# Another written-out order for a kernel of attention and a two-layer product on one core

## The chip, the cores and the metric

The kernel runs on one core of a Trainium2 chip. The metric is device time in microseconds (us) of one execution; a run gives one such time, and a kernel is compared by the median of its runs. The engines of the core are named as in the profile: PE (TensorE matmul, PEld its weight loads), DVE (VectorE), ACT (ScalarE), POOL (GpSimd) and SP (SyncE, which here only issues DMAs).

## The reference

Four batches of eight heads, 768 positions, 64 values a head. Heads 0, 2 and 6 attend causally to everything before them; the other five keep only the first four keys and a window of 64. The attention's output, with the heads side by side, is 3072 rows of 512, and goes through a two-layer product with a slope for negative values:

```
scores = scale * np.matmul(q, k.transpose(0, 1, 3, 2))
...
a = np.exp(scores)
a = a / (np.sum(a, axis=-1, keepdims=True) + 1e-09)
return np.matmul(a, v).astype(np.float32)
...
h = x @ w_in                                      # 512 -> 2048
g = np.maximum(h, 0.0) + alpha * np.minimum(h, 0.0)
return (g @ w_out).astype(np.float32)             # 2048 -> 512
```

## The kernel before

**Units of work.** The heads go two at a time: pair n = 0 to 15 is a batch (n // 4) and two heads of it. The third pair of a batch (n % 4 = 2) has one causal and one windowed head, the last (n % 4 = 3) two windowed ones. Each step of a pair is an item with a name, and the program is one long list of these names, `ORDER` (line 14). The kernel defines all items and then calls them in the order of the list; nothing else schedules. Each engine, and each engine's DMA queue, works its own items off strictly in that order, and waits (on semaphores) where an input or a buffer is not ready. A suffix /V, /A or /P puts an item on DVE, ACT or POOL in place of its default engine.

**The names.** For pair n, with head hh where there are two parts:

- `Lq`, `Lk`, `Lv` load q, k and v to SBUF (lines 189 to 205). All are issued by SP but for one k load, which ACT issues. A q or k load of batch 0 is one head, 128 x 384 float32 (192 KB), in packets of 1.5 KB; a v load is two to five DMAs in packets of 256 bytes, since a row of v is 64 floats.
- `C` casts q and k to bf16 (L323), `Cv` casts v (L328). In batch 0, `T` transposes on PE and `tq`, `tk` copy the result from PSUM. In later batches `tq` and `tk` are transposes of 32 x 32 blocks on DVE, `Dm` parks the result in device memory (L338, four DMAs), and `Dq`, `Dk` fetch it back in the layout that the scores need (L342 to L352); `dk` copies the four first keys.
- `S` are the score matmuls (L442), `s` the exponentials on ACT (L486, L527, L530), `m` the masks by multiplication, `A` the products with v (L556), `a` the division (L565, L566), `X` and `x` the transpose and copy to `xT` (L581).

For block t of the rows (two blocks a batch, 512 and 256 rows): `P` is the first product (L603), `p` and `g` its activation on ACT and DVE (L608, L615), `O` the second product (L623), `o` the copy and the store. `P` of block 0 needs `x` of all four pairs of batch 0, and is cut in parts for its first columns: `P0.4.0` and `P0.5.0` need `x0` and `x1` alone.

`wi0` to `wi7` load w_in as eight DMAs of 64 partitions and 512 columns, `wo0` to `wo3` load w_out as four. These cast from float32 on the way, and POOL issues them on a queue of its own, which the profile names software_dynamic (q0); SP's is q1, hardware_dynamic:

```
def load_w_in(n):
    hh, lo = n % 2, n // 2 * 512
    nc.gpsimd.dma_start(w_in_b[D * hh:D * hh + D, :, lo:lo + 512],
                        dram(moe_w_in, 4 * D * hh * d_ff + lo, [[d_ff, D], [D * d_ff, 4], [1, 512]]))
```

The first columns of `P0` read `wi2` and `wi3`, the next ones `wi4` and `wi5`. Each of POOL's DMAs signals on one of eight semaphores in turn, so the first w_out load can be issued when the first w_in load has landed, the second after the second, and so on. SP's DMAs likewise: each is issued once the one eight before it has landed.

**Warm-up.** `warm` items are matmuls on zeros that only keep PE busy. `Al` turns the slopes on PE.

**Staging.** While PE works on `P` and `O` of batch b, the other engines and PE between these prepare and run the attention of batch b + 1. Only the attention of batch 0 has nothing beside it: until its four `x` are there PE has no `P` to do.

Of the kernel before, what the change touches and what calls it, by code (L numbers as in the profile page):

```python
# [11 lines left out]


ORDER = """
busz busy Lk0.1 kz1 kx1 Lq1.0 warm13 warm10 kx3 warm9 warm4 warm11 Lk0.0 warm1 vo id La Al C0.0.1/P Lk1.0 ey ky1
warm16 Lq0.0 or os1 C0.0.0 Lq0.1 T0.0 C0.1.1/A C0.1.0/A T0.1 m12.1.2 C1.0.0 warm0 tq0.0/V tk0.0/A Lq3.0 warm14 zero st
tq0.1 tk0.1 warm17 Lk2.1 S0.1.2 Lq2.0 warm6 s0.1.2 one Lk2.0 S0.0.2 S0.0.0 s0.0.2 al C2.0.0 S0.1.0 sz1 os2 S0.1.1
Lq3.1 S0.0.1 s0.0.0 s0.0.1 Lq1.1 Lk1.1 s0.1.0 C1.1.0/V T1 tq1/V tk1 Lv3 Lq2.1 S1.0.0 Cv3.1/V s1.0.0 C2.1.0/V T2 Lv0
Cv3.0/V m8.0.2 S1.0.1 s0.1.1 S1.1.0 Cv0/A kx2 s1.0.1 S1.1.1 Lk3.0 tk2.0 tq2 S2.0.0 C3.0.0/A tk2.1 Lq5 nmr s1.1.1
s1.1.0 Lv2 A0.0 Cv2.0 wi3 ky2 kz2 sz2 warm2 ky3 a0.0 S2.0.2 S2.1.0 Lk3.1 C3.1.0 Cv2.1 s2.0.0 T3 wi4 Lv1 Cv1/A tq3 A0.1  # L20
wi2 s2.1.0 S2.0.1 sz0 tk3 wi5 s2.0.2 kz3 S3.1.0 a0.1 s2.0.1 S2.1.1 s2.1.1 A1.1 A2.0 a1.1 A1.0 a1.0 S3.1.1 S3.0.0
s3.1.0 S3.0.1 s3.1.1 s3.0.0 a2.0 A3.1 A2.1 s3.0.1 X1 x1/A Lk5 A3.0 C5.0.0 a3.1 a2.1 X0 warm5 x0 a3.0 warm15 X2 P0.5.0
wi7 X3 x3 x2/A P0.7 P0.9 p0.7 g0.7 p0.9 P0.8 P0.6 g0.9 P1.6 p1.6 g1.6 p0.6 g0.6 P0.10 C5.1.0 tk5 p0.10 P0.11 Lq4 wi1
wi6 p0.11 P0.14 g0.10 tq5 p0.14 g0.14 g0.11 Lk4 P0.13 P0.4.0 P0.5.1 P0.5.2 p0.5 g0.5 Lk7 P1.8 wi0 P0.4.1 P0.4.2 p1.8
P0.12 P0.0.0 P0.0.1 p0.8 g0.8 wo0 g1.8 Lq7 p0.12 g0.12 P0.3.0 P0.0.2 p0.4 P0.3.1 P0.3.2 p0.3 warm8 P0.2.0 C4.0.0
P0.2.1 P1.12 wo1 P0.1.0 Dm5 g0.4 Dq5 P0.1.1 P0.1.2 Dk5 C4.1.0/V nms warm7 p0.13 g0.13 P1.4 g0.3 tq4 tk4 Dm4 P1.10 p0.1
g0.1 C7.1.0/A P1.2 wo2 p0.0 P0.2.2 C7.0.0/V p1.2 g0.0 Dk4 P0.15 Lk6 g1.2 p0.2 g0.2 tk7 P1.14 wo3 P1.0 p1.0 p1.14
O0.3.0 O0.1.0 O0.1.1 Dq4 g1.0 m14.0.2 Lq6 g1.14 p1.10 O0.3.1 tq7 Dm7 p1.12 p1.4 dk5/A S5.0.1 S5.1.2 g1.10 g1.4 O0.3.2
O0.2.0 O0.2.1 O0.2.2 Lv5 s5.1.2 O1.1.0 p0.15 g0.15 S5.1.0 g1.12 S5.0.0 S5.0.2 s5.0.2 O0.2.3 s5.0.0 o0.2/V m5.0.2
s5.1.0 O0.1.2 S4.1.1 S4.1.3 C6.1.0/V S4.0.0 s4.0.0 C6.0.0/V s4.1.1 m4.1.1/P s4.1.3 O0.1.3 m4.0.0/P o0.1 tk6 O0.3.3  # L30
o0.3 tq6 m5.0.0 S4.1.2 S4.0.3 s4.0.3 O0.0.0 S4.1.4 S5.1.1 s4.1.2 m5.1.0 S4.0.1 S4.0.5 Cv5/V s5.0.1 m5.0.1 warm3 m5.1.2
Lv4 s4.0.1 s4.1.4 m4.1.4/P O1.1.1 O1.1.2 s5.1.1 m5.1.1 S4.0.4 S4.1.0 S4.0.2 S4.1.5 s4.1.5 m4.1.5 A5.0 O1.1.3 A5.1 a5.0
m4.0.3 a5.1 Dk7 s4.0.2 O0.0.1 s4.1.0 dk7/P Dq7 S7.1.0 S7.0.2 m4.1.0/P S7.0.1 s4.0.5 S7.0.0 s4.0.4 m4.0.5 o1.1 Dm6
S7.1.2 S7.1.1 Lv7 s7.1.1 s7.1.2 m7.1.2 m7.1.1 Cv4/V m4.0.1/P Dq6 O1.0.0 O1.0.1 s7.1.0 Dk6.0 Dk6.1 dk6/P warm12 s7.0.0
s7.0.1 m4.0.4 O0.0.2 m7.0.0 A4.0 X5 S6.0.1 s7.0.2 S6.0.3 S6.0.4 Cv7 s6.0.1 O1.0.2 a4.0 m6.0.1 x5 S6.1.0 S6.0.2 S6.1.1
m7.1.0 s6.0.4 m6.0.4 s6.0.3 m6.0.3 m4.1.3/P Lq8 S6.1.2 m7.0.1 m7.0.2 S6.0.0 S6.0.5 s6.1.0 s6.1.1 m6.1.0/P Lv6 s6.0.2
A7.1 Cv6.0/P Lk8 a7.1 s6.0.0 m6.0.0/P Lq9 Lq10 A4.1 s6.0.5 a4.1 A7.0 a7.0 O1.0.3 s6.1.2 m6.0.5/P A6.0 X7 Lk9 m6.1.1 X4
m6.1.2 Cv6.1/A A6.1 O0.0.3 x7/A a6.0 a6.1 X6 C8.0.0/V x6 C8.1.0/V tk8 x4/A P2.0 tq8 P2.1 p2.1 P3.2 g2.1 C9.1.0/V P2.15
C9.0.0/V P2.7 p2.15 P3.10 o0.0/V g2.15 o1.0 tq9 P3.12 tk9 P3.6 Dm8 p3.2 p3.12 g3.12 p3.6 g3.6 Lq11 g3.2 P2.3 p2.3 Lk10
g2.3 C10.1.0 C10.0.0/A tk10 P2.9 p2.9 g2.9 p2.0 P3.4 p3.4 P2.4 p2.4 m8.1.2 g2.0 g3.4 p2.7 P2.5 g2.4 P2.13 P3.0 P2.12  # L40
g2.7 p2.13 g2.13 Dm9 tq10 p2.5 Dq8 P2.14 p2.14 g2.14 Lk11 C11.1.0 g2.5 P2.2 Dk8 P2.10 p2.2 g2.2 C11.0.0 tk11 P2.6 Lv9
Lq13 P2.8 O2.2.0 Dk9 p2.6 Dq9 p2.10 p2.8 g2.6 P2.11 p2.11 g2.10 O2.0.0 O2.0.1 g2.8 O2.2.1 tq11 g2.11 O2.0.2 O2.2.2
p3.10 p2.12 Lv10 Lv11 Cv9/P Dm11 p3.0 g3.10 dk9/A S9.1.0 S9.0.2 g3.0 S9.0.0 S9.0.1 S9.1.1 g2.12 Lk13 S9.1.2 s9.1.2
C13.1.0/V m9.1.2/P O2.2.3 s9.0.0 Lq12 s9.1.1 s9.0.2 O2.0.3 s9.1.0 m9.1.0/P o2.0/V s9.0.1 m9.0.1 P3.8 o2.2 S8.0.1
S8.1.5 S8.0.0 S8.0.5 S8.1.3 S8.1.4 p3.8 O2.1.0 s8.1.3 Lk12 O2.1.1 O2.1.2 Lv8 s8.0.5 m8.0.5 g3.8 O2.1.3 Dk11 C13.0.0/A
s8.1.5 m9.0.2/P s8.0.0 S8.0.3 S8.0.4 S8.1.2 m9.0.0 S8.0.2 tq13 S8.1.0 s8.1.4 m8.1.4/P s8.0.1 m8.0.1 S8.1.1 Dq11 dk11/P
O3.1.0 m8.0.0 Cv8/A m9.1.1/P s8.0.4 s8.0.2 o2.1/V A9.0 P3.14 s8.1.2 a9.0 s8.0.3 Dm10 m8.0.4/P Dq10 m8.0.3/P s8.1.1
m4.0.2 s8.1.0 A9.1 S11.0.1 a9.1 S11.1.1 S11.1.0 p3.14 g3.14 S11.0.0 S11.0.2 Cv11/P Dk10.0 tk13 O3.1.1 s11.0.0 s11.0.1
A8.0 C12.0.0/V O3.1.2 Dk10.1 S10.0.3 s11.1.1 dk10 S10.1.0 S10.0.1 Lk15 s11.1.0 s11.0.2 m11.1.0 S11.1.2 C12.1.0/A
S10.0.0 Dm13 S10.1.2 m11.0.1 O3.1.3 s10.0.3 s10.0.1 s10.1.2 a8.0 s11.1.2 s10.1.0 m11.1.1 O3.0.0 m10.0.1 m10.0.3  # L50
S10.1.1 s10.0.0 m10.0.0 m11.1.2 Lq15 S10.0.4 m8.1.1/P S10.0.5 S10.0.2 s10.0.5 m11.0.0/P C15.1.0/A s10.1.1 O3.0.1
s10.0.4 m8.1.0/P m10.1.0 Cv10.0 A11.1 a11.1 s10.0.2 m10.1.1 m8.1.5/P m8.1.3/P A8.1 m11.0.2 O3.0.2 O3.0.3 A11.0 a8.1
Cv10.1/A X9 X8 Lv13 x9/A Cv13/A Lv15 O2.3.0 m10.1.2 A10.1 a11.0 m10.0.4/P m10.0.5/P A10.0 O2.3.1 a10.1 a10.0 O2.3.2 x8
X11 X10 x10/A O2.3.3 x11 tk12 P5.12 tq12 Dm12 o2.3/V C15.0.0/V tk15 P4.8 P4.13 o3.0/V P4.0 Lk14 o3.1 P4.15 p4.15 g4.15
Lq14 P4.10 p4.10 g4.10 p4.8 P4.2 p4.2 tq15 C14.0.0 P4.14 g4.8 p4.0 g4.0 P4.9 C14.1.0 Dk13 P4.1 p4.13 g4.13 p4.1 g4.2
P4.3 p4.3 g4.3 P4.12 g4.1 P4.7 p4.7 g4.7 p4.14 g4.14 P4.5 p5.12 g5.12 p4.5 g4.5 P4.4 p4.4 P5.0 Dq12 g4.4 Dq13 p4.9
g4.9 P4.6 P4.11 p4.12 P5.10 tq14 g4.12 dk13/A Dk12 p4.6 g4.6 p4.11 O4.3.0 g4.11 O4.2.0 O4.2.1 O4.2.2 O4.2.3 p5.0 g5.0
p5.10 S13.0.0 S13.0.1 S13.1.1 S13.0.2 S13.1.2 O4.3.1 O4.3.2 O4.3.3 s13.0.2 s13.1.2 g5.10 s13.0.1 Dm15 Dk15 m10.0.2
dk15/A S12.0.1 S12.1.5 S12.0.0 s13.1.1 tk14 S13.1.0 s13.0.0 s13.1.0 P5.6 m13.1.0/P o4.3/V p5.6 P5.4 p5.4 O4.1.0
s12.0.0 O4.1.1 s12.1.5 O4.1.2 m13.1.2 S12.1.1 m13.0.2 S12.0.2 g5.6 S12.0.3 g5.4 s12.0.1 S12.0.4 S12.1.3 o4.2/V S12.0.5  # L60
m13.0.1 Cv15/P m12.0.0 S12.1.0 s12.0.5 m12.0.5/P s12.0.3 s12.0.2 O4.1.3 m13.0.0 A13.0 O4.0.0 o4.1/V s12.0.4 m13.1.1
s12.1.1 m12.0.4 s12.1.0 a13.0 s12.1.3 Dm14 Dq15 m12.0.3 m12.0.1 m12.1.0 O4.0.1 Dq14 S15.0.0 Lv12 S15.1.1 S15.0.1
S15.0.2 S15.1.2 m4.1.2 Dk14.1 S15.1.0 dk14 Cv12/P A13.1 s15.1.2 s15.0.2 m15.1.2 a13.1 s15.1.0 s15.1.1 m15.1.1 s15.0.1
s15.0.0 O4.0.2 O4.0.3 m12.1.3/P Dk14.0 A12.0 o4.0/V S12.1.4 X13 S12.1.2 S14.0.0 S14.0.3 a12.0 P5.2 P5.14 x13 P5.8
s14.0.3 p5.2 g5.2 s14.0.0 m14.0.0 m15.0.0 s12.1.2 p5.14 g5.14 O5.0.0 O5.0.1 p5.8 g5.8 Lv14 S14.0.4 Cv14.1/P S14.0.1
S14.1.0 m12.1.1 S14.0.5 s12.1.4 Cv14.0/A m15.0.2 m12.1.4/P m12.1.5 S14.1.2 S14.0.2 S14.1.1 s14.1.1 s14.0.2 O5.0.2
s14.0.1 m15.1.0 s14.1.2 m14.0.1 m14.1.1/P A15.1 A12.1 s14.1.0 m14.1.0/P m15.0.1 A15.0 a12.1 m14.0.3/P a15.1 a15.0
s14.0.4 m14.0.4 m14.1.2/P O5.1.0 s14.0.5 O5.1.1 O5.1.2 A14.1 a14.1 m12.0.2 m14.0.5/P A14.0 a14.0 O5.1.3 X15 X12 X14
x12/A x15/A O5.0.3 x14 P6.12 P6.8 p6.12 g6.12 o5.1 p6.8 P7.6 g6.8 P6.11 p6.11 P6.0 P6.1 p6.1 o5.0 g6.1 p7.6 g7.6 P7.4
P6.3 g6.11 P6.14 P7.10 p6.0 g6.0 p7.10 p6.3 P6.6 p6.6 g6.3 g6.6 P6.4 p6.4 p7.4 g7.4 P6.10 p6.14 P6.2 g6.14 p6.2 g6.4  # L70
g6.2 P6.13 P6.9 g7.10 P6.15 p6.9 g6.9 P6.7 p6.15 g6.15 p6.7 g6.7 m6.0.2 P7.14 p6.10 P7.12 P6.5 p6.5 g6.5 O6.3.0 O6.2.0
# [753 lines left out]
```

## Time and profile before

| | us |
|---|---|
| median of 3 runs | 243.77 (242.94 to 243.86) |
| the profiled execution, its own time | 241.82 |
| its span, first to last instruction | 240.1 |
| PE busy in the span | 223.3 (93%) |
| DVE, ACT, POOL busy | 160.6, 137.4, 62.0 |
| PE busy from 0 to 34 us | 26.2 of 34 |
| PE busy from 34 to 127 us | 91.0 of 93 |
| PE busy from 127 to 139 us | 9.7 of 12 |
| PE busy from 139 to 240.1 us | 96.5 of 101.1 |

The table says where a different order can change the time: PE is the engine that is nearly always busy, and what it lacks lies mostly in the first 34 us, with a smaller piece from 127 to 139 us. In the first 34 us it is busy with warm-up too, and partly at a lower clock.

### The profile page before, as it was taken

What the parts mean: (1) busy time and instruction counts of PE and PEld (TensorE: products, weight loads), DVE (VectorE), ACT (ScalarE), POOL (GpSimd) and SP (SyncE); (2) the same over time, 40 slices, a digit from 0 to 9 for tenths busy, and PEclk for the clock granted to TensorE, in tenths of its full rate; (3) what the DMA queues carried; (4) which work ended last, traced back from release to release, by engine and by line L of the source; (5) the groups of instructions that cost most, each with busy time, mean ns of one, the idle gap of its engine ahead of it and who ended that gap; (6) DMA issues with size and microseconds to landing.
All of it is one profiled execution on the core that took longest, in us unless ns stands there. A gap on an engine that the chain in (4) does not pass through costs nothing. (4 is left out here: it accounts for less than half of the span.)

```text
span 240.1 us, 5361 instructions
## 1 busy us (share of the span) xinstructions
PE 223.3 (93%) x1990; PEld 130.3 (54%) x2019; DVE 160.6 (67%) x393; ACT 137.4 (57%) x276; POOL 62.0 (26%) x112
## 2 busy tenths in 40 slices
PE   7778789999999989999998899999999999999993
PEld 2567645575445657544464454454557655456543
DVE  3854555998385898997578576994878654674410
ACT  3476845665386754863998542684587555645101
POOL 2506981000053222140765113120442611000000
PEclk9976999999999999999999999999999999999999
DMA  6999999956998875999977906943761002000222
GB/s 227 289 250 194 289 223 205 207 106 151 273 266 232 204 252 147 308 228 224 296 231 188 209 9 164 310 87 76 199 159 46 0 3 87 1 3 0 98 90 76
DMA packets 65523, 39.67 MB, mean 165 GB/s; under 512 B 48905, under 2 KB 63705, under 8 KB 65497
## 3 DMA queue, kind: packets, MB, share of 16 engines
q1 hardware_dynamic: 59305, 30.01, 49.7%
q0 software_dynamic: 5728, 8.91, 16.2%
q10 hardware_dynamic: 464, 0.40, 0.5%
q8 instruction: 16, 0.26, 0.5%
q14 instruction: 10, 0.08, 0.1%
HBM read 32.50 MB, written 11.01 MB: 181 GB/s over the span
## 5 line engine op out<-in xcount | busy, mean ns | idle before, releaser
L603 PE MATMUL P<-xT,w_in_b 128*128 128x256 bf16 (+1 forms) x503 | 85.3, 325 | 1.5 <-DMA w_in_b<-in_moe_w_in_dram 0.9
L615 DVE SCALAR_TENSOR_TENSOR g<-neg,oma,P 128x256 bf16<-128x256 f32 (+1 forms) x128 | 70.9, 608 | 21.6 <-ACT neg L608 21.3
L623 PE MATMUL P<-w_out_b,g 128*128 128x512 bf16 x350 | 83.7, 379 | 1.3 <-issue 0.5
L608 ACT ACTIVATE neg<-P 128x512 f32<-128x512 f32 x96 | 54.8, 601 | 42.1 <-PE P L603 33.6
L603 PEld LDWEIGHTS <-w_in_b 128*128 128x128 bf16 x512 | 49.6, 98 | 35.8 <-issue 2.5
L623 PEld LDWEIGHTS <-g 128*128 128x128 bf16 x368 | 33.7, 98 | 37.5 <-issue 1.6
L486 ACT ACTIVATE eR<-P 128x448 bf16<-128x448 f32 (+1 forms) x63 | 33.9, 616 | 7.9 <-PE P L442 7.2
L527 ACT ACTIVATE eS<-P 128x368 bf16<-128x368 f32 (+1 forms) x55 | 26.3, 526 | 16.1 <-PE P L442 15.1
L442 PE MATMUL P<-qT,kT 64*128 64x184 bf16 (+7 forms) x272 | 25.2, 256 | 5.3 <-DVE kT L406 1.2
L631 POOL DMA_DIRECT2D out_dram<-ot x18 | 11.5, 639 | 62.9 <-DVE ot L629 46.0
L442 PEld LDWEIGHTS <-kT 64*128 64x128 bf16 x272 | 14.0, 96 | 15.8 <-issue 8.8
L566 DVE TENSOR_TENSOR xn<-P,rcp 128x384 bf16<-128x384 f32 x32 | 17.8, 558 | 1.6 <-PE P L442 0.5
L629 DVE COPY ot<-P 128x512 f32<-128x512 f32 x13 | 8.9, 682 | 14.9 <-PE P L623 14.9
L332 DVE STREAM_TRANSPOSE mid<-nat 128x384 f32<-128x384 f32 x24 | 16.3, 705 | 0.1
L498 POOL TENSOR_TENSOR eR<-eR,mr 128x128 bf16<-128x128 bf16 x27 | 11.7, 447 | 16.2 <-issue 8.2
L538 DVE TENSOR_TENSOR eS<-eS,ms 128x368 bf16<-128x368 bf16 x35 | 11.7, 348 | 5.3 <-ACT eS L527 5.3
L538 POOL TENSOR_TENSOR eS<-eS,ms 128x368 bf16<-128x368 bf16 x10 | 8.9, 889 | 22.6 <-ACT eS L527 22.6
L565 DVE RECIPROCAL rcp<-P 128x6 f32<-128x6 f32 x32 | 6.1, 190 | 9.6 <-PE P L556 9.6
L556 PE MATMUL P<-vb,eS 124*128 124x65 bf16 x240 | 10.6, 193 | 1.3 <-DVE eS L538 1.1
L323 POOL CAST nat<-qkf 128x768 bf16<-128x768 f32 x8 | 7.9, 998 | 15.0 <-DMA qkf<-in_q_dram 7.1
L581 ACT COPY xT<-P 128x768 bf16<-128x768 bf16 x8 | 6.2, 800 | 9.7 <-PE P L442 8.7
L556 PEld LDWEIGHTS <-eS 124*128 124x128 bf16 x240 | 9.2, 97 | 4.0 <-DVE eS L538 1.3
(78 smaller groups left out, 167.4 us busy)
## 6 DMA issues: line engine op xcount, KB each, us to landing
qkf<-in_q_dram SPq DMA_DIRECT2D x12, 384.0 KB
qkf<-in_k_dram SPq DMA_DIRECT2D x12, 384.0 KB
mem<-mid SPq DMA_DIRECT2D x48, 96.0 KB
out_dram<-ot POOLq DMA_DIRECT2D x18, 256.0 KB, 4.0
vf<-in_v_dram SPq DMA_DIRECT2D x19, 210.0 KB
vf<-in_v_dram SPq DMA_DIRECT2D x12, 192.0 KB
qT<-mem SPq DMA_DIRECT2D x12, 192.0 KB
w_in_b<-in_moe_w_in_dram POOLq DMA_DIRECT2D x8, 256.0 KB, 10.5
```

The source lines that it names most:

```text
L332: nc.vector.transpose(words.rearrange("p (w r i) -> p i w r", w=4, i=3), nat[n].bitcast(fp32)[:, S // 2 * x:S // 2 * (x + 1)])
L442: fn(to, x, y, **dict(zip(("start", "stop"), flags)))
L486: nc.scalar.activation(ebuf[n, hh][:, lo:hi].rearrange("p (x c) -> p x c", x=len(parts)), banks(got)[:, 0:len(parts), 0:(hi - lo) // len(p ...
L498: by(n, hh, m).tensor_tensor(ej, ej, mr, op=ALU.mult)
L527: nc.scalar.activation(slots_of(n, hh, m), sc[:, :, 0:2 * WIDE].rearrange("p x (s c) -> p x s c", c=WIDE), AF.Exp, scale=scale)
L538: by(n, hh, m).tensor_tensor(slots, slots, ms[:, first:first + 2 * len(x), :], op=ALU.mult)
L556: nc.tensor.matmul(pav[:, i, :], e[0:rows, o:o + 128], vv[0:rows, j, hh, 0:D + 1], start=(m == 0), stop=(m == len(terms) - 1))
L566: nc.vector.tensor_tensor(in_pairs(xn[n], hh, 3), pav[:, :, 0:D, :], rcp.to_broadcast([128, 3, D, 2]), op=ALU.mult)
L603: nc.tensor.matmul(psg[:, w * i:w * (i + 1)], w_in_b[:, c, 128 * fb:128 * (fb + 1)], xT[:, c, o:o + w], start=(x == 0), stop=(x == 3))
L608: nc.scalar.activation(neg[t, f], bank(held["P", t, f][0]), AF.Relu, scale=-1.0)
L615: nc.vector.scalar_tensor_tensor(g_buf[t % 2][:, fb, 0:w], neg[t, f][:, c], oma[:, fb:fb + 1], bank(got[0])[:, c], op0=ALU.mult, op1=ALU.add)
L623: nc.tensor.matmul(bank(held["O", t, s][0]), g_buf[t % 2][:, f, 128 * s:128 * (s + 1)], w_out_b[:, f, :], start=(f == 0), stop=(f == 15))
```

## The change

Only the list `ORDER` changes, in nearly all its lines; the items, their instructions and their shapes are the same. What it amounts to in each queue up to the start of `P0`:

SP issues, before: Lk0.1 Lq1.0 Lk1.0 Lq0.0 Lq0.1 Lq3.0 Lk2.1 Lq2.0 Lk2.0 Lq3.1 Lq1.1 Lk1.1 **Lv3** Lq2.1 Lv0 Lk3.0 Lq5 **Lv2** Lk3.1 Lv1 Lk5 Lq4 Lk4 Lk7 Lq7.
After: Lk1.1 Lk0.1 Lq0.0 Lq0.1 Lq2.0 Lq1.1 Lq2.1 Lk2.0 Lk1.0 Lq3.0 Lk2.1 Lq1.0 **Lv2** Lk3.1 Lk3.0 Lq3.1 Lv0 Lv1 Lq5 **Lv3** Lk5 Lq4 Lk4, then the first park, Lq7 Lk7.

POOL, before: C0.0.1 C1.0.0 st C2.0.0 nmr Cv2.0 **wi3** C3.1.0 Cv2.1 **wi4 wi2 wi5** C5.0.0 **wi7** C5.1.0 **wi1 wi6 wi0** wo0 C4.0.0 wo1 nms wo2 wo3.
After: st C2.0.0 C1.1.0 C2.1.0 nmr Cv2.0 **wi4 wi3 wi2 wi0 wi1 wi5 wi6 wi7** wo1 wo0 wo2 wo3 C7.1.0 nms.

ACT's casts of v, before: Cv0 after s0.1.1 and Cv1 after s2.0.0. After: none of these two (both on DVE), but tq3 and Cv3.0 between s1.1.0 and s2.0.2.

PE: `Al` comes first, ahead of all warm-up matmuls. Ahead of `X3` stand P0.4.0, P0.5.0 and P0.4.1, before it was P0.5.0 alone.

In later batches `Dm10`, `Dq10` and the q and k loads of batch 3 stand further ahead of their readers, and the cast C15.1.0 goes from ACT to POOL and behind the attention of batch 2. The core of the diff:

```diff
-busz busy Lk0.1 kz1 kx1 Lq1.0 warm13 warm10 kx3 warm9 warm4 warm11 Lk0.0 warm1 vo id La Al C0.0.1/P Lk1.0 ey ky1
...
-Cv3.0/V m8.0.2 S1.0.1 s0.1.1 S1.1.0 Cv0/A kx2 s1.0.1 S1.1.1 Lk3.0 tk2.0 tq2 S2.0.0 C3.0.0/A tk2.1 Lq5 nmr s1.1.1
-s1.1.0 Lv2 A0.0 Cv2.0 wi3 ky2 kz2 sz2 warm2 ky3 a0.0 S2.0.2 S2.1.0 Lk3.1 C3.1.0 Cv2.1 s2.0.0 T3 wi4 Lv1 Cv1/A tq3 A0.1
-wi2 s2.1.0 S2.0.1 sz0 tk3 wi5 s2.0.2 kz3 S3.1.0 a0.1 s2.0.1 S2.1.1 s2.1.1 A1.1 A2.0 a1.1 A1.0 a1.0 S3.1.1 S3.0.0
-s3.1.0 S3.0.1 s3.1.1 s3.0.0 a2.0 A3.1 A2.1 s3.0.1 X1 x1/A Lk5 A3.0 C5.0.0 a3.1 a2.1 X0 warm5 x0 a3.0 warm15 X2 P0.5.0
-wi7 X3 x3 x2/A P0.7 P0.9 p0.7 g0.7 p0.9 P0.8 P0.6 g0.9 P1.6 p1.6 g1.6 p0.6 g0.6 P0.10 C5.1.0 tk5 p0.10 P0.11 Lq4 wi1
...
-S10.0.0 Dm13 S10.1.2 m11.0.1 O3.1.3 s10.0.3 s10.0.1 s10.1.2 a8.0 s11.1.2 s10.1.0 m11.1.1 O3.0.0 m10.0.1 m10.0.3
-S10.1.1 s10.0.0 m10.0.0 m11.1.2 Lq15 S10.0.4 m8.1.1/P S10.0.5 S10.0.2 s10.0.5 m11.0.0/P C15.1.0/A s10.1.1 O3.0.1
...
+kx1 kx3 Lk1.1 busy zero La busz id ey Al Lk0.1 warm1 one Lq0.0 ky1 C0.0.0 warm11 sz2 ky3 Lk0.0 C0.0.1/V Lq0.1 or warm8
...
+sz1 Lv2 s0.1.2 Lk3.1 s0.0.2 Lk3.0 C1.0.0/V T1 tq1/V tk1 tk2.0 S0.1.0 s0.1.0 S1.0.0 S1.1.1 s1.1.1 nmr warm7 Lq3.1
+C3.1.0/A kz3 tq2 tk2.1/A ky2 s1.0.0 Lv0 Cv0/V S1.1.0 S2.0.0 Lv1 S1.0.1 sz0 s1.0.1 warm2 A0.0 warm14 a0.0 C3.0.0/A
+Cv1/V s2.0.0 T3 S2.0.2 S2.1.0 s1.1.0 A1.1 Cv2.0 A0.1 tq3/A Lq5 tk3 wi4 Lv3 Cv3.0/A a1.1 s2.0.2 warm5 wi3 S3.1.0 s2.1.0
+a0.1 kx2 S2.0.1 s2.0.1 wi2 S2.1.1 s2.1.1 A1.0 a1.0 s3.1.0 S3.1.1 Cv2.1/V S3.0.0 Lk5 m12.0.2 s3.0.0 Cv3.1/V A2.0 s3.1.1
+A2.1 a2.1 S3.0.1 warm3 X1 X0 x0/A a2.0 A3.1 wi0 s3.0.1 X2 A3.0 warm4 a3.1 x1/A warm16 P0.4.0 x2 P0.5.0 P0.4.1 C5.0.0/V
...
+s8.0.2 s8.1.5 A9.1 m8.1.5 A9.0 O3.1.0 Cv10.0 a9.0 O3.1.1 s8.1.2 Dk10.0 o2.1 dk11/A S11.0.2 S11.0.1 p3.14 S11.1.0 a9.1
+Dk10.1 S11.1.2 g3.14 S11.1.1 S11.0.0 dk10/P s11.0.2 Dq10 s11.1.1 s11.1.2 m11.1.2 O3.1.2 O3.1.3 s11.0.0 m11.0.0 s11.1.0
...
+Lv15 Cv15/A Lv13 Lv12 p4.3 Dm13 C15.1.0 Cv12/P P5.4 Lq14 C15.0.0/V tq15 p5.4 P4.1 p4.1 g4.1 g5.4 P5.10 g4.3 P4.7 p4.7
```

## The prediction

> **What bounds the kernel now.** I read busy time by stretch first, then the page's slices, POOL's and ACT's timelines in the lead, and the DMA queues in short windows. The stretches:
>
> ```profile
> 0.00:34.00 34.00, 26.20 (x434) 19.08 (x437) 19.30 (x81) 21.24 (x34) 17.26 (x36) 0.90 1.03 248
> 34.00:127.00 93.00, 90.99 (x715) 50.73 (x729) 71.53 (x156) 59.35 (x127) 24.62 (x44) 1.00 0.92 222
> 127.00:139.00 12.00, 9.66 (x102) 5.30 (x102) 7.99 (x25) 8.04 (x18) 3.56 (x8) 1.00 0.82 182
> ```
>
> Columns are the stretch, its length, busy us of PE, PEld, DVE, ACT and POOL, granted clock, DMA share, GB/s. From 34 us on PE is the bound: it lacks 2 of 93 us, then 2.3 of 12. Before 34 us the DMA engines are the full ones (share 1.03), and PE fills time with warm-up. So a new order moves the end by what it does to the lead, the time until the first `P0`, plus what it takes from 127 to 139 us. What gates the lead stands in POOL's and ACT's timelines (start, length, line, and in brackets the idle time before and what ended it):
>
> ```profile
> 10.61 0.30 POOL L225 TENSOR_SCALAR_AFFINE_SELECT mr<-one 128x128 bf16<-128x128 bf16 x1
> 19.69 0.50 POOL L328 CAST vb<-vf 128x384 bf16<-128x384 f32 x1 [8.78 <-DMA vf<-in_v_dram]
> 20.13 0.77 POOL L669 DMA_DIRECT2D w_in_b<-in_moe_w_in_dram  x1
> 23.02 1.84 POOL L669 DMA_DIRECT2D w_in_b<-in_moe_w_in_dram  x3
> ```
> ```profile
> 24.39 0.94 ACT L328 CAST vb<-vf 124x896 bf16<-124x896 f32 x1 [2.11 <-DMA vf<-in_v_dram]
> 31.40 0.80 ACT L581 COPY xT<-P 128x768 bf16<-128x768 bf16 x1
> ```
> ```profile
> 34.02 0.38 PE L603 MATMUL P<-xT,w_in_b 128*128 128x512 bf16 x1 [0.91 <-DMA w_in_b<-in_moe_w_in_dram]
> ```
>
> The cast Cv2.0 holds POOL 8.8 us for Lv2, and w_in stands behind it; its transfers begin when batch 0's loads are nearly in. ACT waits 2.1 us for Lv1 (Cv1), then needs 7.8 us (24.39 to 32.20) for Cv1, eight exponentials of pairs 2 and 3 and x1. `P0` starts at 34.02, 9.6 us after Cv1's start.
>
> How the two DMA queues share the engines shows in three windows, 64 to 66, 28 to 31 and 47.25 to 48.25 us (packets, MB, share):
>
> ```profile
> q1 hardware_dynamic: 1418, 0.42, 87.8%
> ```
> ```profile
> q0 software_dynamic: 331, 0.32, 63.6%
> q1 hardware_dynamic: 333, 0.48, 51.4%
> ```
> ```profile
> q0 software_dynamic: 149, 0.15, 89.1%
> q1 hardware_dynamic: 136, 0.05, 29.7%
> ```
>
> Alone, SP's queue moves 709 small packets a us (mostly v, 256 bytes). Beside w_in or w_out, whose packets are 1 KB, the queues alternate packet for packet, whatever the sizes: 331 to 333 against 1.5 KB loads, 149 to 136 against the 384-byte packets of a park. Small packets then run at 136 to 149 a us, a fifth of their rate. The park of pair 5 paid that: issued at 43.8 to 45.8 us, landed by 51.6; the park of pair 4, issued at 54.6 to 56.0 with POOL's queue empty, landed by 58.1.
>
> **The change, part by part.** *When w_in starts.* Lv2 takes Lv3's place as SP's thirteenth load. By the trace's landings that place was in at 12.15 us. POOL's casts before it are ready for it: C2.0.0, C1.1.0 and C2.1.0 (0.99 us each) follow loads 8 and 11 (in at 8.5 and 10.4), so the last ends at 11.4, and nmr at 11.7. Cv2.0 runs at about 12.1, and the eight w_in DMAs have nothing between them any more: at 0.62 us each they are issued from 12.6 to 17.6, 7.5 us sooner. The first w_in packet came 2.8 us after its issue began (20.13 to 22.9), the next group's 4.0 us (23.02 to 27.05); so POOL's queue flows from 15.4 to 16.6. The w_out DMAs wait only for the first four w_in landings and keep it fed: 8 x 256 + 4 x 512 = 4096 packets.
>
> *What it meets.* Lv2, Lk3.1, Lk3.0 and Lq3.1 are in by 15.0 (load 12 in at 11.1, 1636 small packets at 709 a us, 384 large ones at about 240). Then follow Lv0 (1536 packets), Lv1 (1736), Lq5 (256) and the first head of Lv3 (868): 4396, of which 280 (start at 15.4) to 1130 (16.6) are through. One for one with 4096, at 136 to 149 a us, the remaining 4116 take 27.6 to 30.3 us, the remaining 3266 take 21.9 to 24.0. Lv3's first head lands between 38.5 and 45.7; I take the middle, 42. Before, all v of batch 0 was in by 24.3.
>
> *Who waits.* ACT's new order has Cv3.0 between tq3 and s2.0.2, so ACT stands from about 25 until that landing; queued behind it are the same eight exponentials, x0 and x1, and for them PE (the second products, `X`, `P0`) and DVE. DVE waits likewise in Cv1 (Lv1, about 33 to 38 us) with tk3 behind it, and PE in A1.1; these end before ACT's wait. From Cv3.0 on: before's 7.8 us, less 0.37 (a cast of one head, 0.57 in a later row, for 0.94), plus 0.80 (x0, now on ACT): 8.2. First `P0` at 42 + 8.2 + 0.1 = 50.3, against 34.0: **+16.3**, bounds +12.8 to +20.0.
>
> *Lead pieces.* Before, PE lost 0.6 us between the first `P0` and 36 (X3 and x3). Three pieces instead of one stand ahead of X3: **-0.5** (0 to -0.6).
>
> *Clock.* Before, the clock was 0.51 from 15.3 to 22.2 us, which costs at most half of 6.9. PE would now stand from about 27 to 38 and restart slowly beside ACT: **+1.5** (0 to +3.4).
>
> *Warm-up.* Al first makes PE wait for the slopes (in at 4.26) instead of starting at 1.28, and ACT takes four more copies and a cast early (some 3 us). Nothing: the loads hide both (T0.1 needs loads 2 and 4, in at 4.5 and 6.4; ACT waits later). Without that cover it is 1 to 3 us.
>
> *Batches 1 to 3.* From 127 to 139 us PE lacks 2.3 us and loses 1 more in slow starts. Scores of pair 10 wait for Dk10, and A11.0 for a mask behind ACT's 2.6 us wait for Lq15 (C15.1.0). Dm10 and Dq10 stand some 4 us of PE work sooner and C15.1.0 leaves ACT: **-2.5** (+1 to -3.5; +1 since Dk8, Dk11 and Dk6.1 come close to their scores). Matmul work is unchanged; the score bursts pair their two halves 0.4 us better, in the lead, where it is hidden.
>
> Sum: 16.3 - 0.5 + 1.5 - 2.5 = **+14.8 us**. On the profiled execution's 241.8 (span 240.1 plus 1.7) that is 256.6; the median of the runs is 2.0 higher than that execution, 243.8, and gives 258.6. I predict **257**, between the two. Its own range: +11.3 to +18.5 by the gate, nearly, so 250 to 264.
>
> **Rivals.** *Equal bytes.* If the queues alternated in batches of records rather than record for record, small records would travel together: 16 of 256 bytes (4 KB, 0.36 us an engine at 709 a us over 16 engines) against four of 1 KB (0.31 us at the 210 a us that q0 moved alone from 36 to 42 us). v would run at 382 a us, 4116 take 10.8 us, and Lv3's head lands at 26.2: first `P0` at 34.5, +0.5; with -0.5, +0.5 and -2.5 it is -2.0, 240 to 242. The one-for-one windows speak against it: 384-byte records would have gone ten to four. 12%. The Trainium skill ("DMA: Bandwidth & Descriptors", Queues, rings and completion order) has such a rule: each DMA engine goes round the queues a whole packet at a time, of about 9 to 17 descriptors. By that rule this rival would be the forecast; the trace's 149 to 136 disagrees, if its records are descriptors.
>
> *Faster: SP's queue keeps its rate.* If w_in does not slow the v loads, the 4116 take 5.8 us, Lv3's head is in by 21.3, and ACT is done with x1 about 2.5 us sooner than before: -2.5 - 0.5 - 2.5 = -5.5, 236 to 238. The point that decides is Cv3.0's start: at 28 us, `P0` begins 2.3 us late (28 + 8.3 against 34.0), which -0.5, +0.5 and -2.5 just make good; sooner is a gain. For it: the third pair's k does come 7 us sooner. Against: the three windows. 8%.
>
> *Half.* POOL's transfers start later, since its descriptors are slow to come or Cv2.0 waits for more than Lv2's first head, and fewer packets collide: +1 to +5, 244.5 to 249. In this case the change does not do what it says, w_in is not much sooner. 10%.
>
> **How the numbers follow.** The forecast has 70%. About 0.5% (1.2 us) is what a measurement of this kernel can tell from no change. Faster by more: the fast rival's 8% and most of the equal-bytes case, 0.17; within: 0.04; slower: 0.79. The range 241 to 264 leaves out the fast rival, the better part of equal bytes and a tail above, together just under 20%.
>
> **What the profile after would show.** Right: POOL's w_in DMAs issued from about 12.6 us without a break; from 17 to 37 us equal packets in q0 and q1, with q1 under 200 a us; ACT idle over 10 us ahead of a cast `vb<-vf` of one head (L328), ended by DMA; the first L603 near 50 us; 127 to 139 us's waits for Dk10 and Lq15 gone. Wrong: q1 at 350 or more packets a us beside q0 (equal bytes), no long ACT wait (fast rival), w_in issues near 20 us (half), or a PE that loses several us after the lead at parks and fetches, which I cost at 1 at most.

## The result and the profile after

The kernel after takes 255.5 us (median of 4 runs, 254.83 to 256.65) against 243.81 (4 runs, 242.94 to 245.27) beside it: a ratio of 1.048, with a 95% interval of 1.041 to 1.054. It is slower by 11.7 us; the forecast was 257, range 241 to 264. Single executions of any of these kernels come out 1.5% and more above its fastest, and the medians of the experiments and all ratios leave those out.

The profiled execution after has a span of 253.9 us and a time of 255.6. Its span is 13.8 us longer than that of before; 2 us of the difference to 11.7 are because the profiled execution of before lay 2 us under its median.

Busy time by stretch (columns as in the prediction: stretch, length, busy us of PE, PEld, DVE, ACT and POOL, granted clock, DMA share, GB/s):

```profile
0.00:34.00 34.00, 22.17 (x277) 14.88 (x278) 15.00 (x64) 16.83 (x26) 13.46 (x28) 0.76 1.10 229
34.00:49.00 15.00, 11.01 (x169) 8.90 (x169) 5.37 (x14) 7.59 (x14) 0.00 (x0) 0.64 0.94 192
49.00:142.00 93.00, 90.62 (x696) 49.68 (x704) 69.15 (x157) 60.71 (x130) 25.15 (x40) 1.00 0.68 175
142.00:155.00 13.00, 11.74 (x169) 7.13 (x169) 9.20 (x30) 7.24 (x17) 5.95 (x10) 1.00 1.11 299
```

There is a new stretch of 15 us ahead of the part in which PE is full: the lead, up to the first `P0`, is 13.5 us longer. In it PE runs at 0.64 of its clock. The steady part starts at 49 us and again lacks 2.4 us in 93.

POOL's timeline (start, length, line; the DMA issues of w_in, L669, and w_out, L673):

```profile
11.94 0.50 POOL L328 CAST vb<-vf 128x384 bf16<-128x384 f32 x1
12.39 5.19 POOL L669 DMA_DIRECT2D w_in_b<-in_moe_w_in_dram  x8
19.27 0.76 POOL L673 DMA_DIRECT2D w_out_b<-in_moe_w_out_dram  x1 [1.70 <-DMA w_in_b<-in_moe_w_in_dram]
```

The eight loads of w_in are issued in one go, from 12.4 to 17.6 us. Two windows of the DMA queues, 14 to 16 and 16 to 36 us (packets, MB, share):

```profile
q1 hardware_dynamic: 1427, 0.36, 108.3%
q0 software_dynamic: 65, 0.07, 25.4%
```
```profile
q0 software_dynamic: 3034, 2.96, 89.1%
q1 hardware_dynamic: 2925, 1.08, 31.2%
```

Up to 16 us SP's queue still has the engines, at 714 packets a us. From then on, for 20 us, the two queues move about as many packets each, 3034 to 2925, and SP's queue moves 146 a us. (Whether they take turns packet by packet or in equal groups these counts don't tell; "one for one" below means the counts.) w_in and w_out get nearly three times the bytes in the same number of packets.

ACT's timeline shows who waits for that; only tq3, Cv3.0 and the two copies x0 and x1 are shown:

```profile
25.00 0.82 ACT L389 COPY qT<-P 128x768 bf16<-128x768 bf16 x1
36.07 0.56 ACT L328 CAST vb<-vf 124x448 bf16<-124x448 f32 x1 [10.25 <-DMA vf<-in_v_dram]
...
45.52 0.80 ACT L581 COPY xT<-P 128x768 bf16<-128x768 bf16 x1 [2.54 <-PE P L442]
...
46.73 0.82 ACT L581 COPY xT<-P 128x768 bf16<-128x768 bf16 x1
```

And PE's and DVE's timelines in the same stretch:

```profile
29.82 0.55 PE L442 MATMUL P<-qT,kT 64*128 64x448 bf16 x1
37.51 0.26 PE L442 MATMUL P<-qT,kT 64*128 64x128 bf16 x1 [7.14 <-ACT eR L486]
...
47.52 1.24 PE L603 MATMUL P<-xT,w_in_b 128*128 128x512 bf16 x5
```
```profile
42.67 0.42 DVE L328 CAST vb<-vf 124x448 bf16<-124x448 f32 x1 [1.13 <-DMA vf<-in_v_dram]
```

ACT stands 10.2 us for the first head of Lv3, PE 7.1 us for the exponential behind it, and the first `P0` comes at 47.5 us, where it came at 34.0. DVE waits a second time, for Lv3's second head. Behind the first `P0` nothing is gained or lost: the span that is left is 206.4 us after and 206.1 before, and PE is busy 197.2 and 197.1 us of it.

### The profile page after: what moved, and what is told of

Its sections match the earlier page's. It is cut to its first block, busy times and chain, and to the rows that moved or that the text cites. A ratio compares the mean times of both kernels' runs of the same rounds, so it can differ in the third digit from the quotient of the medians.

```text
span 253.9 us, 5366 instructions
## 1 busy us (share of the span) xinstructions
PE 228.9 (90%) x1992; PEld 133.5 (53%) x2019; DVE 158.0 (62%) x392; ACT 143.3 (56%) x286; POOL 60.3 (24%) x103
## 5 line engine op out<-in xcount | busy, mean ns | idle before, releaser
L603 PE MATMUL P<-xT,w_in_b 128*128 128x512 bf16 (+1 forms) x505 | 85.9, 325 | 0.4
L615 DVE SCALAR_TENSOR_TENSOR g<-neg,oma,P 128x512 bf16<-128x512 f32 (+1 forms) x128 | 70.9, 605 | 20.4 <-ACT neg L608 19.9
L603 PEld LDWEIGHTS <-w_in_b 128*128 128x128 bf16 x512 | 49.8, 98 | 35.4 <-issue 1.1
L442 PE MATMUL P<-qT,kT 64*128 64x184 bf16 (+6 forms) x272 | 26.8, 263 | 11.9 <-ACT eR L486 7.1
L323 POOL CAST nat<-qkf 128x768 bf16<-128x768 f32 x13 | 12.7, 994 | 59.6 <-DMA qkf<-in_k_dram 52.7
L631 POOL DMA_DIRECT2D out_dram<-ot x18 | 11.5, 639 | 51.7 <-DVE ot L629 36.3
L629 DVE COPY ot<-P 128x512 f32<-128x512 f32 x11 | 7.4, 682 | 20.2 <-PE P L623 20.2
L566 DVE TENSOR_TENSOR xn<-P,rcp 128x384 bf16<-128x384 f32 x32 | 17.8, 557 | 1.1
L538 DVE TENSOR_TENSOR eS<-eS,ms 128x368 bf16<-128x368 bf16 x36 | 13.2, 383 | 4.7 <-ACT eS L527 4.3
L498 DVE TENSOR_TENSOR eR<-eR,mr 128x128 bf16<-128x128 bf16 x38 | 10.1, 301 | 6.2 <-ACT eR L486 6.1
L629 ACT COPY ot<-P 128x512 f32<-128x512 f32 x12 | 7.2, 603 | 12.0 <-remote 7.9
L556 PE MATMUL P<-vb,eR 128*128 128x65 bf16 x252 | 11.4, 206 | 0.8 <-DVE eR L498 0.6
```

What stands on the lines that cost most here:

```text
L442: fn(to, x, y, **dict(zip(("start", "stop"), flags)))
L538: by(n, hh, m).tensor_tensor(slots, slots, ms[:, first:first + 2 * len(x), :], op=ALU.mult)
L556: nc.tensor.matmul(pav[:, i, :], e[0:rows, o:o + 128], vv[0:rows, j, hh, 0:D + 1], start=(m == 0), stop=(m == len(terms) - 1))
L566: nc.vector.tensor_tensor(in_pairs(xn[n], hh, 3), pav[:, :, 0:D, :], rcp.to_broadcast([128, 3, D, 2]), op=ALU.mult)
L603: nc.tensor.matmul(psg[:, w * i:w * (i + 1)], w_in_b[:, c, 128 * fb:128 * (fb + 1)], xT[:, c, o:o + w], start=(x == 0), stop=(x == 3))
L615: nc.vector.scalar_tensor_tensor(g_buf[t % 2][:, fb, 0:w], neg[t, f][:, c], oma[:, fb:fb + 1], bank(got[0])[:, c], op0=ALU.mult, op1=ALU.add)
```

## Experiments

Each kernel was timed beside the order before on the same chip; ratios are to it, with a 95% interval in brackets. "First P0" is the start of the first L603 matmul in the profile.

The theory: w_in's packets lie beside the v loads, which then run at a fifth of their rate; ACT waits for the last of them in Cv3.0, and PE's half clock stretches what follows. Rivals: the new places of Lv3 in SP's queue and of Cv3.0 in ACT's make the loss by themselves; or the later batches do.

### 1. w_in sooner, alone (order before)

```diff
-... nmr s1.1.1 s1.1.0 Lv2 A0.0 Cv2.0 wi3 ... wi4 ... wi2 ... wi5 ... wi7 ... wi1 ... wi6 ... wi0
+... nmr wi4 wi3 wi2 wi0 wi1 wi5 wi6 wi7 s1.1.1 s1.1.0 Lv2 A0.0 Cv2.0 ...
```

> The order before, with w_in alone sooner: its eight loads stand behind the mask nmr and ahead of Cv2.0 on POOL, so that they are issued from 11 us on instead of from 20.1 to 33. All other queues keep their order, w_out follows as it did. Theory of sharing: q0 flows from some 14 us, the v loads of pairs 0 to 3 that were in by 24.3 us run at some 150 packets a us, land 6 to 10 us later, and the first P0 comes at 40 to 45 us instead of 34; the time 249 to 254 us instead of 243.8. Rival, w_in sooner costs nothing by itself (it takes the new places of the v loads and casts as well): 242 to 245.

Measured: 251.02 us (2 of 4 runs), ratio 1.032 [1.017, 1.047]. The profile, first POOL, then ACT, PE, and the DMA queues from 22 to 28 us:

```profile
11.00 5.08 POOL L669 DMA_DIRECT2D w_in_b<-in_moe_w_in_dram  x8
27.33 0.50 POOL L328 CAST vb<-vf 128x384 bf16<-128x384 f32 x1 [11.25 <-DMA vf<-in_v_dram]
```
```profile
34.53 0.94 ACT L328 CAST vb<-vf 124x896 bf16<-124x896 f32 x1 [11.49 <-DMA vf<-in_v_dram]
```
```profile
43.19 0.38 PE L603 MATMUL P<-xT,w_in_b 128*128 128x512 bf16 x1
```
```profile
q0 software_dynamic: 952, 0.92, 90.3%
q1 hardware_dynamic: 943, 0.25, 30.3%
```

Nothing but w_in's issue moved, and ACT waits 11.5 us in Cv1, the first `P0` comes 9.2 us late, and the time rises by 7 to 8 us (4 to 11 by the interval, since only two executions count). The queues share one for one (952 to 943) here too. The rival in which w_in sooner is harmless without the other moves falls.

### 2. The order after, with w_in and w_out behind the v loads

```diff
-... Cv2.0 A0.1 tq3/A Lq5 tk3 wi4 Lv3 Cv3.0/A a1.1 ... wi3 ... wi2 ... Cv3.1/V A2.0 ...
+... Cv2.0 A0.1 tq3/A Lq5 tk3 Lv3 Cv3.0/A a1.1 ... Cv3.1/P wi4 wi3 wi2 wi0 wi1 wi5 wi6 wi7 wo1 wo0 wo2 wo3 A2.0 ...
```

> The order after, with one thing changed: all loads of w_in and w_out stand on POOL's queue behind the cast of Lv3's second head (Cv3.1, which moves from DVE to POOL for that), so that no record of theirs can lie beside a v load. SP's and ACT's orders stay. Theory of sharing (the v loads are late because w_in's records take every other turn, and ACT waits for the last of them): Lv0, Lv1, Lq5 and both heads of Lv3 run at some 700 small packets a us and are in by 21 to 23 us, ACT's wait ahead of Cv3.0 falls from 10.2 us to under 1, the first P0 comes at 32 to 36 us instead of 47.5, and the time falls from 255.5 to 238 to 243 us; w_in starts at some 23 us and must be there for P0 by its own late start, which is the risk (to 245). Rival, the places in the queues (Lv3 as the twentieth load of SP and Cv3.0 at the head of ACT make the loss by themselves): ACT's wait stays several us, 250 us or more. Rival, the later batches cost it: within 2 us of 255.5.

Measured: 243.59 us (9 of 10 runs), ratio 1.000 [0.996, 1.004]. The DMA queue of SP from 14 to 20 us (no other data queue has packets there), then POOL, ACT and PE:

```profile
q1 hardware_dynamic: 3926, 1.32, 115.7%
```
```profile
25.28 5.09 POOL L669 DMA_DIRECT2D w_in_b<-in_moe_w_in_dram  x8
```
```profile
25.16 0.61 ACT L328 CAST vb<-vf 124x448 bf16<-124x448 f32 x1
```
```profile
34.14 1.24 PE L603 MATMUL P<-xT,w_in_b 128*128 128x512 bf16 x5
...
39.05 8.12 PE L603 MATMUL P<-xT,w_in_b 128*128 128x256 bf16 x37 [2.23 <-DMA w_in_b<-in_moe_w_in_dram]
```

SP's queue runs at 654 packets a us, ACT doesn't wait for Lv3 at all, and the first `P0` is back at 34.1 with Lv3 still twentieth and Cv3.0 still on ACT: the whole loss of the lead goes with the place of w_in and w_out, and the rival of the places falls. The time came out a little above the 238 to 243 expected, by the risk named there: w_in is now issued from 25.3 us, and PE stands 2.2 us for it at 39 (in an execution 2.5 us above the median).

### 3. The order after, with w_in and w_out behind the cast of Lv1

```diff
-... Lv1 S1.0.1 ... Cv1/V s2.0.0 ... A1.1 Cv2.0 A0.1 tq3/A ... wi4 Lv3 Cv3.0/A ...
+... Lv1 S1.0.1 ... Cv2.0 Cv1/P wi4 wi3 wi2 wi0 wi1 wi5 wi6 wi7 wo1 wo0 wo2 wo3 s2.0.0 ... A1.1 A0.1 tq3/A ... Lv3 Cv3.0/A ...
```

> The order after, with all loads of w_in and w_out held on POOL behind the cast of Lv1 (Cv1, moved from DVE to POOL) only, so that w_in is issued at some 19 to 21 us and flows from 22 to 24, beside the last part of Lv3 at most. Theory of sharing: Lv0 and Lv1 are in by 19 to 20 us, Lv3's first head by 22 to 25, second head by 24 to 29; ACT hardly waits, first P0 at 31 to 35 us, the time 237 to 241 us: no slower than the kernel before. Rival, the places in the queues: 250 us or more.

Measured: 241.25 us (7 of 10 runs), ratio 0.994 [0.988, 0.999]. POOL, and PE from the first `P0` on:

```profile
20.68 5.08 POOL L669 DMA_DIRECT2D w_in_b<-in_moe_w_in_dram  x8
```
```profile
34.22 1.24 PE L603 MATMUL P<-xT,w_in_b 128*128 128x512 bf16 x5
35.73 15.67 PE L603 MATMUL P<-xT,w_in_b 128*128 128x512 bf16 x86
```

With w_in issued at 20.7 us its first packet runs at 23.4, behind all of batch 0's v, and PE goes through the first products without the stop of experiment 2. The time lies just above the 237 to 241 expected. This is as fast as the order before or slightly faster (0.1 to 1.2%), some 14 us faster than the order after, with one cast on another engine and twelve DMA issues in another place.

### 4. The order after, with w_out alone held back

```diff
-... Cv2.0 ... wi4 Lv3 ... wi7 ... wo1 ... wo0 ... wo2 wo3 ... Cv3.1/V A2.0
+... Cv2.0 wi4 wi3 wi2 wi0 wi1 wi5 wi6 wi7 ... Lv3 ... Cv3.1/P wo1 wo0 wo2 wo3 A2.0
```

> The order after, with w_out alone held back: its four loads stand behind Cv3.1 on POOL (moved there from DVE), the eight of w_in stay where they are. Theory of sharing: w_in's 2048 packets keep the queue busy until some 32 us, as after, and only then is SP's queue alone; what is left of Lv3 by then, some 600 packets of the first head and 870 of the second, moves at 700 a us instead of 155. First head at 33 to 33.5 instead of 36.0, second at 34.5 instead of 42.6; ACT's wait 2.5 to 3 us shorter, first P0 at 43.5 to 45 instead of 47.5, the time 251 to 253 us. Rival, equal shares do not come from the number of w_in's and w_out's packets but from SP's own order: within 1 us of 255.5.

Measured: 251.91 us (4 runs), ratio 1.037 [1.033, 1.041]. ACT, PE, and the DMA queues from 31 to 34 us:

```profile
33.65 0.56 ACT L328 CAST vb<-vf 124x448 bf16<-124x448 f32 x1 [7.10 <-DMA vf<-in_v_dram]
```
```profile
44.38 1.24 PE L603 MATMUL P<-xT,w_in_b 128*128 128x512 bf16 x5
```
```profile
q1 hardware_dynamic: 1627, 0.72, 109.5%
q0 software_dynamic: 46, 0.04, 7.6%
```

When w_in runs out at some 31 us SP's queue is at once back at over 500 packets a us, and Lv3's first head comes 2.4 us sooner. The first `P0` is 3.1 us sooner and the time 3.6 us shorter. This is what was expected of sharing: the loss goes with the number of packets on the other queue.

### 5. The order after, with Cv3.0 behind the exponentials on ACT

```diff
-... tq3/A Lq5 tk3 wi4 Lv3 Cv3.0/A a1.1 s2.0.2 ... s3.1.1 ...
+... tq3/A Lq5 tk3 wi4 Lv3 a1.1 s2.0.2 ... s3.1.1 Cv3.0/A ...
```

> The order after, with Cv3.0 on ACT moved behind the exponential s3.1.1: eight exponentials no longer stand behind the wait for Lv3's first head. All loads stay as late as after. Theory (late loads, and ACT is only the first to feel them): the exponentials run from 26 us on, but PE's A3.1 and DVE's Cv3.1, which stand ahead of the second and later X and of P0, still wait for Lv3's second head at 42.6, so the first P0 comes at 44 to 46 instead of 47.5 and the time falls by 2 to 4 us, to 251.5 to 253.5. Rival, ACT's place in the queue is the cause by itself: first P0 at 34 to 37, the time 242 to 245.

Measured: 256.5 us (4 runs), ratio 1.056 [1.052, 1.059]: no gain, where 2 to 4 us were expected. DVE and PE:

```profile
42.15 0.43 DVE L328 CAST vb<-vf 124x448 bf16<-124x448 f32 x1 [9.42 <-DMA vf<-in_v_dram]
```
```profile
43.31 0.58 PE L442 MATMUL P<-ident_f,xn 64*128 64x64 f32 x6 [7.17 <-DVE xn L566]
...
46.80 2.24 PE L603 MATMUL P<-xT,w_in_b 128*128 128x512 bf16 x5
```

The expectation was right that Lv3's second head becomes the bound, and wrong about how much that leaves. DVE stands 9.4 us in Cv3.1, with the division behind it that X0 needs, and PE 7.2 us for that. PE's clock was 0.50 from 40 to 48 us, so the five matmuls that take 1.24 us after take 2.24 here. The first `P0` gains 0.7 us, and what follows it takes 1.4 us more (span 254.6).

### 6. The order after, with both casts of Lv3 on POOL

```diff
-... Lv3 Cv3.0/A a1.1 s2.0.2 ... Cv3.1/V A2.0 ...
+... Lv3 a1.1 Cv3.0/P s2.0.2 ... Cv3.1/P A2.0 ...     (w_in and w_out issued ahead of both)
```

> The order after, with both casts of Lv3 (Cv3.0 from ACT, Cv3.1 from DVE) on POOL behind the issues of w_in and w_out, where nothing waits behind them before 45 us. The loads stay as late as after. Moving Cv3.0 alone left DVE waiting 9.4 us in Cv3.1 with the division ahead of X0 behind it. Theory (late loads; each engine that holds such a cast only feels them): with neither ACT nor DVE held, the exponentials and divisions of pairs 0 to 2 end by 36 us, x0 at 37 to 38 instead of 43.9, but PE stands in A3.1, ahead of the first P0 in its queue, until Lv3's second head is in at 41.7 and cast at 42.3; first P0 at 43.5 to 45 and then at half clock for some us: 252 to 255 us. Rival, the casts' places in ACT's and DVE's queues are the cause: first P0 by 38, 245 to 248.

Measured: 254.33 us (4 runs), ratio 1.046 [1.042, 1.051]. ACT's x0, then PE:

```profile
35.80 0.80 ACT L581 COPY xT<-P 128x768 bf16<-128x768 bf16 x1 [1.17 <-PE P L442]
```
```profile
43.47 0.82 PE L556 MATMUL P<-vb,eS 124*128 124x65 bf16 x12 [7.71 <-POOL vb L328]
46.22 2.22 PE L603 MATMUL P<-xT,w_in_b 128*128 128x512 bf16 x5
```

ACT's x0 now comes at 35.8 us, 9.7 sooner than after, and it brings 1.3 us at the first `P0` (46.2, where 43.5 to 45 was expected): PE stands 7.7 us in A3.1 for Lv3's second head, and starts `P0` at half clock. Experiments 5 and 6 moved the wait from ACT to DVE and from DVE to PE; experiments 2 to 4, which moved the landing, moved the end.

### 7. The order after, with PE kept busy in the waits

```diff
-... T3 S2.0.2 S2.1.0 s1.1.0 A1.1 ... s2.0.2 warm5 wi3 S3.1.0 ...
+... T3 S2.0.2 warm18 S2.1.0 s1.1.0 A1.1 ... s2.0.2 warm5 warm19 wi3 S3.1.0 ...     (12 and 30 matmuls)
```

> The order after, with 42 more warm-up matmuls on zeros (12 ahead of the second scores burst of pair 2, 30 ahead of the wait for Lv3's head), which keep PE busy through its waits of 2.3 and 7.1 us; the burst of pairs 2's scores is not interleaved any more, which lies in a wait. If PE's half clock from 27.7 to 44.8 us comes from standing still and stretches the chain from Cv3.0 to the first P0 (11.5 us where 8.2 were expected): the clock stays full from 24 us on, the chain takes 8 to 9 us, first P0 at 44.5 to 45.5 instead of 47.5, the time 252 to 254 us. If the half clock is not PE's waiting, or the chain is bound by ACT and DVE: 30 matmuls at 0.43 us end behind the landing at 36 us, and the time is 255 to 259.

Measured: 252.84 us (4 runs), ratio 1.038 [1.035, 1.041]. The stretches 26 to 36 and 36 to 46 us of the order after, then of this kernel (columns as above), and this kernel's DVE at Cv3.1, ACT at x0 and PE at the first `P0`:

```profile
26.00:36.00 10.00, 2.79 (x35) 1.88 (x35) 2.87 (x10) 0.00 (x0) 0.00 (x0) 0.59 1.21 210
36.00:46.00 10.00, 8.45 (x139) 7.41 (x138) 2.92 (x8) 6.05 (x11) 0.00 (x0) 0.56 1.12 237
```
```profile
26.00:36.00 10.00, 10.00 (x88) 5.30 (x87) 2.77 (x10) 0.42 (x1) 0.47 (x1) 1.00 1.21 211
36.00:46.00 10.00, 8.10 (x166) 6.11 (x165) 4.43 (x12) 6.95 (x14) 0.00 (x0) 1.00 1.15 238
```
```profile
42.17 0.43 DVE L328 CAST vb<-vf 124x448 bf16<-124x448 f32 x1 [2.28 <-DMA vf<-in_v_dram]
```
```profile
43.78 0.80 ACT L581 COPY xT<-P 128x768 bf16<-128x768 bf16 x1 [2.85 <-PE P L442]
```
```profile
45.77 1.24 PE L603 MATMUL P<-xT,w_in_b 128*128 128x512 bf16 x5
```

The clock is full in both stretches, and the time falls by 2.7 us by the medians (the first `P0` by 1.75 us in the profiled execution, the slowest of the four): the half clock comes from PE's standing still, and it costs 1.75 to 2.7 us. The chain from Cv3.0 (35.58) to the first `P0` (45.77) takes 10.2 us instead of 11.45, not the 8 to 9 expected: the eight exponentials end at 40.9, and then ACT waits 2.9 us, because DVE's Cv3.1 comes at 42.2 as in experiment 5, when Lv3's second head is in. The late load is a bound of its own even at full clock.

### 8. The lead of the order before with the rest of the order after

```diff
+(all items of the order after ahead of P0.4.0, in the order and on the engines of before, with the loads of w_in)
 P0.4.0 x2 P0.5.0 P0.4.1 a3.0 X3 x3 P0.6 P1.8 P0.7 ...     (the order after)
```

> The lead of the order before (everything up to the first P0 in the order and on the engines of before, the loads of w_in with it) and the rest of the order after: the later part of the change alone. From the traces' sums of PE's waits (12.9 us behind the first P0 before, 13.2 after) the later part is worth nothing: first P0 at 33.5 to 35, the time 242.5 to 245. The prediction's own term for it was -2.5 us: 240 to 242. Rival, the later part costs part of the loss: 246 or more.

Measured: 243.70 us (8 of 10 runs), ratio 0.997 [0.992, 1.003]. The later part of the change is worth nothing that can be measured, and the rival of the later batches falls. The -2.5 of the prediction would have given 241.3 here (243.83 beside it), and the interval's lower end is 241.8. This run alone doesn't rule the -2.5 out: the lead is that of before only nearly (three of its first warm-up items stand later), and in the profiled execution, 2.0 us above the median, the first `P0` came at 36.7 us, not at the 33.5 to 35 expected. Whether it is as late in the other executions was not seen. But the spans behind the first `P0`, 206.1 us before and 206.4 after, show no such gain either.

### 9. Experiment 3 with Cv3.0 on POOL

```diff
-... Cv2.0 Cv1/P wi4 wi3 wi2 wi0 wi1 wi5 wi6 wi7 wo1 wo0 wo2 wo3 ... Lv3 Cv3.0/A ...
+... Cv2.0 Cv1/P wi4 wi3 wi2 wi0 wi1 wi5 wi6 wi7 ... Lv3 Cv3.0/P wo1 wo0 wo2 wo3 ...
```

> The version with w_in and w_out behind the cast of Lv1, and Cv3.0 moved from ACT to POOL, between w_in's and w_out's issues: ACT gets rid of a cast of 0.61 us that stands ahead of the exponentials, and nothing waits for that load on ACT. Expected 0.3 to 0.6 us under the version without it, 240.5 to 242, so 1 to 2 per cent under the order before at most; within 0.2 us of the former if PE's half clock (20 to 26.5 us) sets the lead instead of ACT.

Measured: 241.26 us (7 of 11 runs), ratio 0.991 [0.987, 0.995]. The median is that of experiment 3 (241.25), the ratio is 0.3% lower, and the two intervals overlap: a gain of the 0.3 to 0.6 us expected can be neither shown nor excluded, and whether the cast of 0.61 us on ACT or PE's half clock sets the lead there stays open. It has the lowest ratio, 0.5 to 1.3% under the order before, but is not told apart from experiment 3.

## Why the prediction was right, point by point

| | predicted | measured |
|---|---|---|
| w_in issued | 12.6 to 17.6 us | 12.4 to 17.6 |
| SP's rate beside it | 136 to 149 a us | 146 |
| Lv3's first head | 42 (38.5 to 45.7) | 36.0 |
| from there to the first `P0` | 8.3, and 1.5 for the clock | 11.5 |
| first `P0`, against 34.0 | +17.8 (16.3 and 1.5) | +13.5 |
| behind it | -0.5 and -2.5 | +0.3 |
| sum | +14.8 | +13.8 in the spans |

**The mechanism held.** Equal numbers of packets from both queues, v at a fifth of its rate and a long ACT wait in Cv3.0 are in the trace of after, and experiments 1 and 2 show both directions: w_in sooner alone costs 7 to 8 us, and w_in and w_out behind v take the loss away.

**Equal bytes** was excluded by 3034 packets of some 1 KB against 2925 mostly of 256 bytes. The Trainium skill ("DMA: Bandwidth & Descriptors", Queues, rings and completion order) has each engine drain a whole packet of some 9 to 17 descriptors before it changes queues. The prediction took this for the rule of equal bytes, and that doesn't follow: turns of equally many records from either queue give equal counts too, as in the order after and in experiment 1 (952 to 943). The counts exclude turns of equal bytes; turns of one record and turns of several they can't tell apart, so they neither confirm nor contradict that rule. **Faster** needed Cv3.0 before 28 us; it came at 36.07. **Half** needed later issues; they came 0.2 us sooner than worked out.

**The gate was 6 us too late**, below the range given for it. The rate was right; the count was not. The step that failed is "280 (start at 15.4) to 1130 (16.6) are through": SP's queue moved 2925 packets from 16.0 to 36.0, when the head landed, so at least 4396 - 2925 = 1471 were through at 16. It moved 1427 packets from 14 to 16 us, and q0 only 65. At 146 a us, 341 packets more than the upper count are 2.3 us. The rest of the 6 is the choice of the middle of the range. (Counted by size in the trace, 1868 were through at 16: the loads ahead of them were in by 14 us, where 15.0 was worked out. Of the 2925, 307 are packets of Lv3's second head and 90 others that the working leaves out, so two errors of count partly cancel.)

**The way behind the landing was priced too short.** From the landing on, 8.3 us were expected and 1.5 more for the clock; it took 11.5. Experiment 7 puts the half clock at 1.75 us at the first `P0` and 2.7 us of the median, inside the bounds of 0 to 3.4; at full clock the way still took 10.2 us. The rest is a step that the prediction left out: it followed ACT's wait for the first head and gave no price to the second, 6 us behind it at the same rate. That head holds DVE's Cv3.1 and PE's A3.1, and experiments 5, 6 and 7 all stop there; without ACT's wait the first `P0` would have gained only 0.7 to 1.3 us.

**Behind the first `P0`** the prediction had -3.0 and there was +0.3. What PE waited for there, before from 36 us and after from 49.5 us on (us in total, times, longest):

```profile
PE P L556 <- DVE eS L538: 1.1, 1, 1.1
PE P L442 <- DVE xn L566: 0.9, 4, 0.3
PE P L442 <- DVE kT L358: 0.5, 1, 0.5
```
```profile
PE P L442 <- DMA qT<-mem: 1.8, 2, 1.1
PE P L556 <- ACT eR L486: 0.9, 1, 0.9
PE P L556 <- DVE eR L498: 0.6, 1, 0.6
```

The waits for the mask and for dk10's copies (L538, L358) are gone, as said. In their place PE waits 1.8 us for two parks fetched back (`qT<-mem`, ahead of the scores of pairs 7 and 10; pair 10 now waits 1.1 us for its q) and 1.5 us for exponentials and masks elsewhere. The step took a gain in one place and looked for new waits only among pairs 8, 11 and 6, at 1 us. The -0.5 for the lead pieces was too large as well: before, PE was busy 1.81 of the 2.00 us from 34 on, so it stood 0.2 us there and not 0.6; after, it is busy for all of the first 2 us.

The lead came out 4 us too long and the rest 3 us too short. That the 257 stood 1.5 us from the median is in part luck, because these two errors point in opposite directions.

## What to carry to other kernels

Before a large load is issued sooner, look which small-packet loads are still in flight at that time: where the trace shows two queues moving equal numbers of packets, the small packets pay (here 146 a us in place of 654 to 714), and here whoever waited for the last of them set the end. Issue the large load behind the landing of the loads that gate the start, as late as its first reader allows: here 20.7 us, where 12.4 cost 14 us and 25.3 made the reader wait 2.2 (in the times, 241.25 and 243.59, the intervals of these last two still overlap). Moving a cast that waits for a late load from engine to engine gained 1.2 us at most here; follow the load's second part, too, to all its readers.

## What was not expected of the hardware

The software queue starts softly: after POOL's first issue at 12.4 us it moved 65 packets up to 16, and was level with SP's queue only from about 20 us, by one-us windows (62, 114, 133, 174, 169, 158 packets a us from 15 on, against SP's 524, 165, 290, 71, 103, 149). In experiment 2 it had the engines to itself and was slow at first too: 126, 138, 109 and 123 packets in the one-us windows from 27 on, then 182 and 184. So the slow start is not the other queue's doing. In both kernels the rate rose when POOL's burst of eight issues had ended (17.6 and 30.4 us); whether that is the cause was not tried.

PE's clock fell to a half at 27.7 us, when PE had just stood for 2.3 us, and came back at 44.8, though PE had been busy for 7.29 of the 7.30 us since 37.5, mostly with short score matmuls. The Trainium skill ("TensorE: Matmul & The Clock Gate", Part 1: The HAM clock gate) gives about 3.4 us of sustained work for the return; this trace shows twice that. Why the matmuls here need longer was not tried.
